# A new order table for an attention and channel-mix kernel: one batch's k'v in single PSUM banks, and a planner that keeps VectorE and GpSimd apart

## The chip, the cores and the metric

The kernel runs on one core of one Trainium2 chip. The metric is the device time of one execution in microseconds (us), the median of three runs; less is better. The time before is 196.96 us (196.91 to 197.13).

## The reference

For each of 8 batches and 8 heads, with 576 rows of 64 columns: q is put through a softmax along its 64 columns, k through a softmax along its 576 rows, then kv = k'v (64x64 for each head) and x = q kv. The heads are laid side by side to rows of 512 columns. Then comes a channel mix:

```
xk = mu_k * x + (1 - mu_k) * x_prev        # x_prev is x, one row later
xr = mu_r * x + (1 - mu_r) * x_prev
k  = max(xk @ w_k, 0)                      # 512 -> 1024
v  = (k * k) @ w_v                         # 1024 -> 512
out = v / (1 + exp(-(xr @ w_r)))           # w_r: 512 -> 512
```

Inputs and output are float32; the matrix products run in bf16.

## The kernel before, in words

The eight heads of a batch are worked on as two **units** of four heads, so "(1,0)" below is unit 0 of batch 1. The steps for a unit are: load q, k and v (L338, SP's queue); exponentials of q and k on ScalarE (L344); v to bf16 (`cast_v`, L349); the row sums of q with a reciprocal (`sum_q`, L354) and the multiply by it (`scale_q`, L359), both on VectorE; the transpose of q; k'v on TensorE (`kv`, L385, 36 small products over 64 rows that add up in PSUM); then x.

Batches 0 and 1 take a way of their own. Their q is transposed on TensorE (L370) and copied out by ScalarE or VectorE (L377). Their k'v is scaled by the normaliser and by mu in `weigh_kv` (L401, on VectorE, in two calls w=0 and w=1, of which the first also takes the reciprocal of the normalisers), and the "mixed" products (`x_mixed`, L411) give xk and xr at once. There are four of these for each unit, and each is copied out by ScalarE or VectorE (L432). From batch 2 on q is transposed by a DMA (L381), k'v is normalised in `norm_kv`, and xk and xr are made by ScalarE and VectorE (L451, L456).

The channel mix has 8 "up" steps for each batch (`up`, L463: a block of 128 columns of w_k; for batches 0 and 1 each is cut into four quarter steps of two products), a relu (L471) and a square (L476); for each block of 128 rows a "gate" (`gate`, L484, with w_r), a tanh (L490) and a "down" (`down`, L500, with w_v), and `finish` (L507) and a store.

The weights come in as float32 and are cast to bf16: w_k in eight column blocks (`cast_wk`, L322), w_r in two halves (`cast_wr`, L326), w_v in four (`cast_wv`, L329), each on ScalarE, VectorE or GpSimd, through one helper (L248), so that all casts and copies have the lines L250 (ScalarE) and L251 (VectorE, GpSimd).

PSUM has 8 banks: three double tiles of two banks ("two", L204) for k'v, transposes, mixed and up products, and two single banks ("one", L205) for gate and down products.

The order of the work is fixed by hand, in the table `ORDER` (L21). Each word is a step's number; a letter behind it chooses the engine (A ScalarE, D VectorE, G GpSimd) where there is a choice. The class `Plan` (L57) goes through the table, reckons a start for each step from costs written beside the steps (L552 on), gives out the PSUM and SBUF buffers (the one that is free first), and the steps are issued in the order of these starts. So the table sets the order on each engine and on SP's queue; on the chip every engine then runs its list in order and waits on semaphores. A step with `shares` set is one that the planner takes to be slower when a VectorE and a GpSimd step run at one time (L107 to L115).

The steps are written down once each, and each has one number in both tables.

Of the kernel before, what the change touches and what calls it, by code (L numbers as in the profile page):

```python
# [21 lines left out]
0 2 1 3 4 7 8 9 10 11 76 96 80 12 13 81 82 6 100 79G 5 77 78A 85 101 86 83A 87 102 14 104D 84A  # L22
88 97 98A 103A 99G 28 105 90 89A 91A 92 17G 93A 106 16G 108 107 114 109A 110 112 115A 365 366
15G 18D 111A 19 113D 27 24 367 136 378 379 368 373 376 377 29 369 371 21G 380 372 22G 374 140
375 94 95D 362 363 23A 30 360 361 393 400 32 394 141 31 364 398 401 20G 33 382 116 399 395 402
384 370D 383 385 396 120 387 389 386 397 390 381A 25D 121 34 388 26G 391 142 37 143D 118D 138D
574 584 40 122 123D 117 119G 575 139G 125 124A 585 126 144D 127 579 569 137 130 131A 128 129A
145 146 147 134 36D 135A 132 148 150 43 133A 426 428 149A 427 431 392D 41 151A 433 429 432 403D
434 404 570 406 407 430 405 444 435 442 38G 408 445 39G 580 420 42 422 411 35D 156 412 423 45
421 409 159 410 576 424 436A 415 417 443 413 173 439 157 160 440 577 418 44 176 437 438 446 441  # L30
586 46 416 177 158 571 419 587 175 154 162 447D 152 174 572 155A 581 613 190 163 425D 153A 161
414D 614 164 179 193 615 582 166 178 589 590 165 47 595 180 168 591 578 169 596 49 597 51 601
602 583 50 170 167 603 194 181 616 172 48 598 171 617 186 187 182 188 183 184 607 191 207 608
609 209 192 463 189 55 464 465 185 210 195 466 458 460 448 57 629 56 588 208 467D 211 461 599
459 462D 453 241 450 449 451 196 454 212 244 197 245 624 630 625 213 214 198 243 200 600 592 199
54 452D 455 204 53 201 593 202 610 634 203 206 456 205 611 242 215 52 635 221 457D 247 619 220
223 620 217 594 216 621 222 58 618 218 219 248 225 631 224 470 471 480 246 227 612 632 468 481
469 478 573 622 228 258 623 261 475 639 476 644 479 640 645 249 250 251 252 226 230 604 253 255
229 636 482A 473 231 254 474 257 605 485 649 256 486 65 650 64 232 637 61 262 233 238 626 472D
483 627 237 239 234 235 63 240 633 484 659 654 59 277 62 236 500 66 487D 275 278 60 292 501 498  # L40
499 495 477A 493 660 488 655 263 294 279 280 494 496 497D 259 489 293 661 503 295 504 490 491
662 276 296 505 628 298 260 299 264 265 492D 651 506 68 266 268 652 281 267 664 507D 641 282 665
674 606 272 638 269 663 271 270 642 675 273 274 283 284 285 286 67 288 656 646 657 289 290 679
291 502D 647 309 74 287 73 508 312 520 509 343 346 521 510 310 511 523 515 643 516 669 512D 680
525 347 297 658 69 311 513 524 514 313 670 526 681 315 300 75 344 305 684 306 316 682 518 70 302
685 666 307 72 301 345 519 314 308 648 667 671 694 527A 522A 695 304 317 71 303 328 318 349 672
689 683 517D 319 690 320 323 322 350 326 676 321 696 324 677 530 327 545 325 528 673 546 543 529
329 348 544 540 531 699 533 697 698 678 534 330 532D 538 704 541 539 700 351 332 333 356 691 705
653 706 535 357 358 352 692 353 536 724 707 331 725 359 714 715 547D 537A 334 354 668 335 542D
701 355 702 708 336 337 711 339 340 341 342 726 555 560 727 709 556 710 338 558 757 729 758 712  # L50
703 561 730 565 559 566 759 563 734 564 735 567D 693 548 553 550 719 760 551 554 557D 549 552D
720 721 728 722 723 713 716 717 718 562A 736 731 737 686 732 738 733 687 744 745 739 749 740 741
688 750 761 568 754 742 743 755 746 747 756 748 751 752 753
# [3 lines left out]
class Plan:  # L57
# [8 lines left out]
    TURN, SHARE = 0.25, {"DVE": 0.45, "POOL": 0.7}  # L66
# [7 lines left out]
    def step(self, eng, cost, fn=None, after=(), uses=(), lat=0.12, narrow=False, shares=False):  # L74
# [81 lines left out]
def kernel(  # L156
# [12 lines left out]
    nc = tc.nc  # L169
# [10 lines left out]
    PARTS = ((0, 5), (5, 4))  # L180

# [54 lines left out]
    def at(kind, *key):  # L236
        return bufs[kind][slot[(kind, *key)]["idx"]]
# [146 lines left out]

    def kv(b, u):  # L385
        ps, ek, vb = at("two", "kv", b, u), at("ek", b, u), at("vb", b, u)
        for j in range(J):
            for g in range(2):
                for h in range(2):
                    r = slice(64 * g, 64 * g + 64)  # L390
                    nc.tensor.matmul(ps[64 * h:64 * h + 64, g, 0:65],  # L391
                                     lhsT=ek[r, j, 64 * h:64 * h + 64], rhs=vb[r, j, h, :],
                                     start=(j == 0), stop=(j == J - 1))
# [7 lines left out]
    def weigh_kv(b, u, w):  # L401
        ps, rz, rows = at("two", "kv", b, u), inv_k(b, u), slice(2 * w, 2 * w + 2)
        if w == 0:
            nc.vector.reciprocal(out=rz, in_=ps[:, :, 64])
        for g in range(2):
            nc.vector.scalar_tensor_tensor(
                out=at("kvm", b, u)[:, rows, g, :], scalar=rz[:, g:g + 1],
                in0=ps[:, g, None, 0:64].to_broadcast((128, 2, 64)),
# [174 lines left out]
    for a in range(2):  # L583
        queue.append(dma(2.85, lambda a=a: load_wk(a), after=early[-1:], uses=[sl("k2", "w")]))
        for c in range(4):
# [3 lines left out]
                shares=True)  # L589
# [3 lines left out]
                        uses=[sl("xr", "w")], shares=True) for c in range(2)]  # L593
# [3 lines left out]
    for a in range(2):  # L597
        first.append(dma(2.75, lambda a=a: load_wv(a), uses=[sl("k2", "w")],
                         after=[*queue, *(ev["wk", i] for i in range(FT))]))
        for c in (2 * a, 2 * a + 1):  # L600
            ev["wv"].append(pl.step({"POOL": 1.2, "ACT": 1.05, "DVE": 0.62}, 0,
                                    lambda e, c=c: cast_wv(e, c), after=[first[-1]],
                                    uses=[sl("k2", "w")], shares=True))
# [6 lines left out]
    for n in range(B):  # L610
        for u in range(2):
# [5 lines left out]
            if n < NM:  # L617
# [4 lines left out]
                              shares=True)  # L622
                      for h in range(2)]
            else:
                vc = [pl.step("POOL", 1.3, lambda n=n, u=u: cast_v("POOL", n, u),
                              after=[ev["ld", "v", n, u]], uses=[vb, sl("ldv", n, u)],
                              shares=True)]
            p = pl.step("DVE", 1.57, lambda n=n, u=u: sum_q(n, u), after=[qe], uses=[eq])
            p = pl.step("DVE", 1.32, lambda n=n, u=u: scale_q(n, u), after=[p], uses=[eq, qs],
                        shares=True)  # L630
            if n < NM:
                s = sl("two", "qt", n, u)
# [8 lines left out]
            s = sl("two", "kv", n, u)  # L641
            p = pl.step("PE", T_NARROW, lambda n=n, u=u: kv(n, u), after=[ke, *vc],
                        uses=[ek, vb, s], lat=0.3, narrow=True)
            if n < NM:
                km = sl("kvm", n, u)
                nk = [p, ev["mu"]]
                for w in range(2):
                    nk.append(pl.step("DVE", 0.75 - 0.2 * w, lambda n=n, u=u, w=w: weigh_kv(n, u, w),
                                      after=nk, uses=[s, km, sl("mub")], lat=0.18))
                weighed += nk[2:]  # L650
                for w in range(2):
                    for c in range(2):
# [11 lines left out]
                         uses=[s, kn], lat=0.35)  # L664
# [15 lines left out]
    for b in range(B):  # L680
        relus = []
        for f in range(FT):
# [14 lines left out]
            if f % 2:  # L697
# [3 lines left out]
                                              lat=0.2, shares=True)  # L701
# [167 lines left out]
```

## Time and profile before

| | before |
|---|---|
| median of three runs | 196.96 us (196.91 to 197.13) |
| the profiled execution | 198.4 us |
| its span, first to last instruction | 196.6 us |
| mean granted TensorE clock | 0.991 |
| last link of the chain that ended last | the last down products on TensorE from 188.93 us, 3.65 us long, then VectorE, 0.42 us |

The profile comes from one execution of its own, so its span and the median of the runs are not the same time. Times in a timeline are microseconds from the span's start. A timeline row gives start, length, engine, line, operation, what is written and read, how many instructions, and in brackets how long the engine stood idle before it and what it waited for. PE is TensorE, DVE VectorE, ACT ScalarE, POOL GpSimd, SP the engine that issues most DMAs. Instructions of one engine overlap a little, so a row can start before the one ahead of it has ended.

### The profile page before, as it was taken

How to read it: one execution, taken by the hardware profiler on the slowest of the kernel's cores; microseconds unless marked ns; L12 is line 12 of the kernel's file. 1: busy time of each engine (PE TensorE's matmuls, PEld its weight loads, DVE VectorE, ACT ScalarE, POOL GpSimd, SP SyncE). 2: the span in 40 equal slices, each digit the busy share in tenths (PEclk: the TensorE clock that was granted, in tenths of full speed). 3: DMA queues.
4: the chain of work that ended last, by engine and by line, in shares of the span. 5: the costliest groups of instructions: out<-in, count | busy, mean ns of one | idle time of the engine just before them, and what ended most of it. 6: DMA issues, size and time to landing. Idle time of an engine off the chain costs nothing. (4 is left out here: it accounts for less than half of the span.)

```text
span 196.6 us, 4720 instructions
## 1 busy us (share of the span) xinstructions
PE 186.3 (95%) x1905; PEld 111.9 (57%) x1905; DVE 145.1 (74%) x225; ACT 144.7 (74%) x214; POOL 30.3 (15%) x40
## 2 busy tenths in 40 slices
PE   6699699999999999999999999999999999999991
PEld 4467475765546754665566645754576546664441
DVE  1984996669999997985997898998791688225222
ACT  3898779897799798887899686979956692752210
POOL 2024731533002312000115000152000000000000
PEclk9879999999999999999999999999999999999999
DMA  5999999994899999949995999948809325104824
GB/s 203 374 398 387 388 391 386 391 390 118 200 327 357 282 264 401 280 106 317 391 350 115 273 285 299 324 153 175 229 19 170 88 53 137 28 0 104 187 71 127
DMA packets 35896, 46.86 MB, mean 238 GB/s; under 512 B 16280, under 2 KB 16544, under 8 KB 35872
## 3 DMA queue, kind: packets, MB, share of 16 engines
q1 hardware_dynamic: 35456, 46.02, 77.8%
q10 hardware_dynamic: 416, 0.53, 1.0%
q8 instruction: 15, 0.25, 0.5%
q14 instruction: 9, 0.07, 0.1%
HBM read 33.56 MB, written 9.44 MB: 219 GB/s over the span
## 5 line engine op out<-in xcount | busy, mean ns | idle before, releaser
L467 PE MATMUL two<-xk,wk_bf 128*128 128x288 bf16 x512 | 66.8, 286 | 1.7 <-POOL wk_bf L251 1.7
L503 PE MATMUL one<-wv_bf,k 128*128 128x512 bf16 (+1 forms) x296 | 65.9, 374 | 0.1
L467 PEld LDWEIGHTS <-wk_bf 128*128 128x128 bf16 x512 | 49.8, 98 | 18.6 <-POOL wk_bf L251 2.0
L472 ACT ACTIVATE rel<-two 128x576 bf16<-128x576 f32 x64 | 40.2, 654 | 22.0 <-PE two L467 19.7
L503 PEld LDWEIGHTS <-k 128*128 128x128 bf16 x296 | 28.1, 98 | 31.0 <-issue 0.6
L486 PE MATMUL one<-wr_bf,xr 128*128 128x512 bf16 x144 | 35.9, 379 | 0.1
L251 POOL CAST vb<-ldv 128x1152 bf16<-128x1152 f32 (+1 forms) x16 | 19.8, 1237 | 92.2 <-DMA ldv<-in_v_dram 91.9
L453 ACT ACTIVATE aw<-two,om 128x575 bf16<-128x575 f32 x48 | 32.5, 748 | 1.5 <-PE two L445 1.5
L491 ACT ACTIVATE th<-one 128x512 f32<-128x512 f32 x36 | 21.5, 604 | 13.4 <-PE one L486 13.4
L509 DVE SCALAR_TENSOR_TENSOR ot<-th,one 128x512 f32<-128x512 f32 x33 | 22.2, 675 | 7.7 <-PE one L503 6.8
L360 DVE TENSOR_TENSOR qs<-eq,inv 128x1152 bf16<-128x1152 bf16 x16 | 25.6, 1607 | 0.2
L355 DVE TENSOR_REDUCE rs<-eq 128x18 f32<-128x1152 bf16 x16 | 21.5, 1346 | 5.2 <-ACT eq L345 5.1
L482 DVE TENSOR_TENSOR k<-rel 128x1152 bf16<-128x1152 bf16 x24 | 18.1, 766 | 8.2 <-ACT rel L472 8.2
L458 DVE SCALAR_TENSOR_TENSOR xk<-two,mu,aw 128x576 bf16<-128x576 f32 x24 | 19.3, 812 | 6.1 <-ACT aw L453 6.0
L486 PEld LDWEIGHTS <-xr 128*128 128x128 bf16 x144 | 13.5, 98 | 13.7 <-issue 0.9
L345 ACT ACTIVATE eq<-ldq 128x1152 bf16<-128x1152 f32 x16 | 18.6, 1170 | 2.7 <-DMA ldq<-in_q_dram 2.6
L458 DVE SCALAR_TENSOR_TENSOR xr<-two,mu,aw 128x576 bf16<-128x576 f32 x24 | 19.2, 810 | 1.4 <-ACT aw L453 1.4
L345 ACT ACTIVATE ek<-ldk 128x1152 bf16<-128x1152 f32 x16 | 18.9, 1181 | 0.0
L480 ACT ACTIVATE k<-rel 128x1152 bf16<-128x1152 bf16 x8 | 9.3, 1180 | 0.0
L333 PE MATMUL one<-ident 128*128 128x256 bf16 x31 | 6.8, 381 | 1.8 <-DVE halves L271 1.8
L391 PE MATMUL two<-vb,ek 64*64 64x65 bf16 x576 | 8.1, 197 | 0.1
L391 PEld LDWEIGHTS <-ek 64*64 64x64 bf16 x576 | 6.7, 110 | 2.3 <-issue 1.1
(56 smaller groups left out, 86.8 us busy)
## 6 DMA issues: line engine op xcount, KB each, us to landing
ldq<-in_q_dram SPq DMA_DIRECT2D x16, 576.0 KB, 7.1
ldk<-in_k_dram SPq DMA_DIRECT2D x16, 576.0 KB, 7.0
out_dram<-ot SPq DMA_DIRECT2D x66, 128.0 KB, 2.7
ldv<-in_v_dram SPq DMA_DIRECT2D x14, 576.0 KB, 7.7
k<-in_moe_w_k_dram SPq DMA_DIRECT2D x2, 1024.0 KB, 12.9
k<-in_moe_w_v_dram SPq DMA_DIRECT2D x2, 1024.0 KB, 12.5
ldv<-in_v_dram SPq DMA_DIRECT2D x4, 288.0 KB, 8.6
xr<-in_moe_w_r_dram SPq DMA_DIRECT2D x1, 1024.0 KB, 14.2
```

Source lines behind the costliest of these rows:

```text
L251: return {"DVE": nc.vector, "POOL": nc.gpsimd}[eng].tensor_copy(out=out, in_=in_)
L345: nc.scalar.activation(out=at("e" + n, b, u)[:].rearrange("p j (h d) -> p h j d", h=2), in_=at("ld" + n, b, u)[:].rearrange("p h (j d) -> ...
L355: nc.vector.reduce_sum(out=rs[:], in_=at("eq", b, u)[:].rearrange("p j (h d) -> p (j h) d", h=2), axis=AX.X)
L360: nc.vector.tensor_tensor(out=at("qs", b, u)[:].rearrange("p j (h d) -> p (j h) d", h=2), in0=at("eq", b, u)[:].rearrange("p j (h d) -> p ...
L453: nc.scalar.activation(out=at("aw", b, u, h, w)[:, 1:S], in_=x_of(b, u, h)[:, 1:S], func=ACT.Copy, scale=om[:, c:c + 1])
L458: nc.vector.scalar_tensor_tensor(out=blend(b, w)[:, 2 * u + h, :], in0=x_of(b, u, h)[:, 64:64 + S], scalar=mu[:, c:c + 1], in1=at("aw", b, ...
L467: nc.tensor.matmul(ps[:, a, 0:HS], lhsT=wk_bf[:, ct, 128 * f:128 * f + 128], rhs=xk[:, ct, HS * a:HS * a + HS], start=(ct == 0), stop=(ct ...
L472: nc.scalar.activation(out=at("rel", b, f // 2)[:, f % 2, :].rearrange("p (a c) -> p a c", a=2), in_=at("two", "up", b, f)[:, :, 0:HS], fu ...
L486: nc.tensor.matmul(at("one", "rp", i, m)[:], lhsT=at("xr", i)[:, ct, 128 * m:128 * m + 128], rhs=wr_bf[:, ct, :], start=(ct == 0), stop=(c ...
L491: nc.scalar.activation(out=at("th", i, m)[:], in_=at("one", "rp", i, m)[:], func=ACT.Tanh, scale=0.5)
L503: nc.tensor.matmul(at("one", "vp", i, m, a)[:, cols], lhsT=at("k2", i)[:, f, 128 * m:128 * m + 128], rhs=wv_bf[:, f, cols], start=(f == 0) ...
L509: nc.vector.scalar_tensor_tensor(out=at(kept(i, m), i, m)[:, cols], in0=at("th", i, m)[:, cols], scalar=1.0, in1=at("one", "vp", i, m, a)[ ...
```

## The change

There are three edits. First, the k'v of unit 1 of batch 1 goes to the two single banks in place of one double tile, a bank for each pair of heads; the reciprocal of its two normalisers is then two instructions in place of one:

```diff
+    KV_SINGLE = (1, 1)
...
+    def kv_of(b, u, g):
+        if (b, u) == KV_SINGLE and ("one", "kv", 0) in slot:
+            return bufs["one"][g][:, 0:65]
+        return at("two", "kv", b, u)[:, g, 0:65]
...
     def weigh_kv(b, u, w):
...
+        if w == 0 and (b, u) != KV_SINGLE:
+            nc.vector.reciprocal(out=rz, in_=at("two", "kv", b, u)[:, :, 64])
+        elif w == 0:
+            for g in range(2):
+                nc.vector.reciprocal(out=rz[:, g:g + 1], in_=ps[g][:, 64:65])
```

Second, in the planner, a VectorE and a GpSimd step of the sharing kind no longer slow each other by a share of their common time; the later one in the table starts when the other has ended. Only the last sharing step of each engine is looked at:

```diff
-    TURN, SHARE = 0.25, {"DVE": 0.45, "POOL": 0.7}
+    TURN = 0.25
...
-            if s["shares"] and e in sharing:
+            if e in s["shares"]:
                 sharing[e], other = s, sharing["POOL" if e == "DVE" else "DVE"]
-                both = min(other["end"], t + cost) - max(other["start"], t) if other else 0.0
-                if both > 0.0:
-                    cost += self.SHARE[e] * both
-                    longer = self.SHARE[other["on"]] * both
+                if other and other["start"] <= t:
+                    t = max(t, other["end"])
+                elif other and other["start"] < t + cost:
+                    longer = t + cost - other["start"]
                     other["cost"] += longer
                     other["end"] += longer
                     busy[other["on"]] += longer
```

The casts of v for batches 0 and 1 now count as sharing on GpSimd only. Third, the table is a new one. Of its 762 steps none is added or dropped. These are the two orders where the first batches are worked on (x is a mixed product, weigh the two calls w=0 and w=1, "exp q (1,0)" the exponential of q).

| engine | before | after |
|---|---|---|
| TensorE, up products of batch 0, in quarter steps | blocks 1, 3, 2, then x (0,0) w=1 c=1, 0, then 6, 7, 4, 5 mixed | all x of batch 0 first; blocks 0, 2, 3, 1, then 7 three times, 6, 7, 5, 6, 6, 6, 5, 5, 5, 4 four times |
| TensorE, from there to the up products of batch 1 | transposes (1,1), gates 1, 3, transposes (1,0), k'v (1,0), gates 2, 0, two x of (1,0), k'v (1,1), two x of (1,0), two x of (1,1) | gates 0, 3, transposes (1,0), gate 1, k'v (1,0), gate 2, transposes (1,1), two x of (1,0), k'v (1,1), two x of (1,0), two x of (1,1) |
| VectorE, same stretch | w_k block 3, copy of x, sum (1,1), copy of x, multiply (1,1), square, sum (1,0), half of w_r, multiply (1,0), copy of q, two casts of v, copy of q, weigh (1,0) around a copy of q, weigh (1,1), quarter of w_v, two squares, quarter of w_v | w_k block 3, two copies of x, w_k blocks 7 and 4, sum and multiply (1,0), half of w_r, sum and multiply (1,1), cast of v, two copies of q, weigh (1,0), two copies of q, weigh (1,1) w=0, copy of x, square, quarter of w_v, weigh (1,1) w=1, square |
| GpSimd | v, v, w_k blocks 2, 1, 0, 5, 6, 4, half of w_r, v, v, two quarters of w_v | v, v, v, w_k blocks 1, 0, 5, 6, half of w_r, v, v, v, three quarters of w_v |
| ScalarE, w_k | block 7 | block 2 |
| SP's loads | q (1,1), w_k second half, q (1,0), w_r, k, v (1,0), v, k, v (1,1), w_v first, second half | q (1,0), w_k second half, q (1,1), w_r, k, v (1,0), k, v, v (1,1), w_v second, first half |

Behind that stretch the order of up, gate, down and k'v steps, of squares (some on the other of ScalarE and VectorE) and of stores, loads and DMA transposes on SP's queue differs in many places. Counted by step, VectorE has 178 before and 179 after, ScalarE 211 and 209, GpSimd 27 and 28. TensorE's 64-row steps (k'v, x, mixed) stand in 20 runs in both tables: 15 of them behind the first up products of batch 1 before, 16 after.

More of the change, by code (lines that the diff above doesn't have):

```diff
@@ L28 @@
[L28 to L33, printed above, removed]
@@ L72, in slot, with step @@
         return {"kind": kind, "users": 0, "idx": None, "end": 0.0}
-    def step(self, eng, cost, fn=None, after=(), uses=(), lat=0.12, narrow=False, shares=False):
+    def step(self, eng, cost, fn=None, after=(), uses=(), lat=0.12, narrow=False, shares=()):
         s = {"eng": eng if isinstance(eng, dict) else {eng: cost}, "fn": fn, "lat": lat,
@@ L401, in weigh_kv @@
     def weigh_kv(b, u, w):
-        ps, rz, rows = at("two", "kv", b, u), inv_k(b, u), slice(2 * w, 2 * w + 2)
-        if w == 0:
-            nc.vector.reciprocal(out=rz, in_=ps[:, :, 64])
+        ps, rz, rows = [kv_of(b, u, g) for g in range(2)], inv_k(b, u), slice(2 * w, 2 * w + 2)
+        if w == 0 and (b, u) != KV_SINGLE:
[3 more added lines that the diff above has]
+                nc.vector.reciprocal(out=rz[:, g:g + 1], in_=ps[g][:, 64:65])
         for g in range(2):
@@ L592 @@
                         lambda e, c=c: cast_wr(e, c), after=[queue[-1]],
-                        uses=[sl("xr", "w")], shares=True) for c in range(2)]
+                        uses=[sl("xr", "w")], shares=("DVE", "POOL")) for c in range(2)]
     first = [ld(n, 1, u, early[-1:]) for n, u in (("q", 0), ("q", 1), ("k", 0), ("v", 0), ("k", 1))]
@@ L640 @@
                              uses=[qs, qT], lat=3.3)]
-            s = sl("two", "kv", n, u)
+            if (n, u) == KV_SINGLE:
+                kv_at = [sl("one", "kv", g) for g in range(2)]
+            else:
+                kv_at = [sl("two", "kv", n, u)]
             p = pl.step("PE", T_NARROW, lambda n=n, u=u: kv(n, u), after=[ke, *vc],
-                        uses=[ek, vb, s], lat=0.3, narrow=True)
+                        uses=[ek, vb, *kv_at], lat=0.3, narrow=True)
             if n < NM:
@@ L647 @@
                 for w in range(2):
-                    nk.append(pl.step("DVE", 0.75 - 0.2 * w, lambda n=n, u=u, w=w: weigh_kv(n, u, w),
-                                      after=nk, uses=[s, km, sl("mub")], lat=0.18))
+                    nk.append(pl.step("DVE", (0.92 if (n, u) == KV_SINGLE else 0.75) * (1 - w) + 0.55 * w, lambda n=n, u=u, w=w: weigh_kv(n, u, w),
+                                      after=nk, uses=[*kv_at, km, sl("mub")], lat=0.18))
                 weighed += nk[2:]
```

78 lines of the change are left out of this document (42 added, 36 removed).

## The prediction

> **What bounds the kernel now.** I read the page first, then busy time by stretches, then the timelines of the engines where TensorE is not full.
>
> ```profile
> span 196.6 us, 4720 instructions
> ...
> PE 186.3 (95%) x1905; PEld 111.9 (57%) x1905; DVE 145.1 (74%) x225; ACT 144.7 (74%) x214; POOL 30.3 (15%) x40
> ```
>
> ```profile
> 17.00:24.00 7.00, 5.25 (x56) 3.67 (x46) 5.35 (x7) 5.76 (x9) 3.57 (x5) 1.00 1.05 387
> 24.00:35.60 11.60, 11.38 (x196) 7.62 (x195) 9.60 (x20) 9.44 (x15) 2.86 (x4) 1.00 1.05 388
> 35.60:47.00 11.40, 11.40 (x84) 7.83 (x82) 7.93 (x10) 10.33 (x15) 6.02 (x4) 1.00 0.92 331
> 47.00:68.00 21.00, 20.86 (x225) 11.94 (x223) 20.83 (x30) 18.66 (x27) 2.50 (x2) 1.00 0.93 265
> ...
> 100.00:150.00 50.00, 50.00 (x521) 30.86 (x520) 42.99 (x61) 40.58 (x60) 7.97 (x5) 1.00 0.80 215
> ```
>
> The columns are length, busy PE, PEld, DVE, ACT, POOL, clock, DMA share, GB/s. From 35.6 us on TensorE has no hole worth naming (11.40 of 11.40, 20.86 of 21.00, 50.00 of 50.00), at full clock. So a new order can win almost nothing there. It can win in the stretch 17 to 24 (5.25 of 7.00), and it can lose anywhere. The timeline of TensorE around that hole:
>
> ```profile
> 20.54 1.15 PE L467 MATMUL two<-xk,wk_bf 128*128 128x288 bf16 x8
> 23.42 4.09 PE L467 MATMUL two<-xk,wk_bf 128*128 128x288 bf16 x32 [1.73 <-POOL wk_bf L251]
> 27.35 0.67 PE L374 MATMUL two<-ident,qs 128*128 128x128 bf16 x9
> 27.86 1.89 PE L486 MATMUL one<-wr_bf,xr 128*128 128x512 bf16 x8
> 29.58 0.67 PE L374 MATMUL two<-ident,qs 128*128 128x128 bf16 x9
> 30.21 0.48 PE L391 MATMUL two<-vb,ek 64*64 64x65 bf16 x36
> 30.70 2.00 PE L486 MATMUL one<-wr_bf,xr 128*128 128x512 bf16 x8
> 32.63 0.69 PE L423 MATMUL two<-qT,kvm 64*64 64x256 bf16 x20
> 33.27 0.48 PE L391 MATMUL two<-vb,ek 64*64 64x65 bf16 x36
> 33.73 0.41 PE L423 MATMUL two<-qT,kvm 64*64 64x256 bf16 x8
> 34.32 1.29 PE L423 MATMUL two<-qT,kvm 64*64 64x320 bf16 x32 [0.18 <-ACT xk L250]
> 35.59 0.65 PE L467 MATMUL two<-xk,wk_bf 128*128 128x288 bf16 x4
> ```
>
> At 21.69 TensorE stops for 1.73 us until GpSimd has cast a column block of w_k. Then it runs the second half of batch 0's up products, and from 27.35 the transposes, gates 0 to 3 and batch 1's first mixed products. At 35.59 batch 1's up products begin. Both tables put the same 59 TensorE steps ahead of that point. So I measure the change there: **the start of batch 1's up products, 35.59 now.** TensorE is full from there to the end, and a shift of that start passes into the time one for one.
>
> The wait has its cause on two engines. GpSimd's rows, then VectorE's:
>
> ```profile
> 15.58 0.87 POOL L251 CAST wk_bf<-k 128x512 bf16<-128x512 f32 x1 [2.03 <-DMA k<-in_moe_w_k_dram]
> 20.99 0.61 POOL L251 CAST wk_bf<-k 128x512 bf16<-128x512 f32 x1 [3.43 <-DMA k<-in_moe_w_k_dram]
> 21.55 1.82 POOL L251 CAST wk_bf<-k 128x512 bf16<-128x512 f32 x1
> 25.19 1.04 POOL L251 CAST wr_bf<-xr 128x1024 bf16<-128x1024 f32 x1 [0.74 <-DMA xr<-in_moe_w_r_dram]
> ```
>
> ```profile
> 15.55 0.43 DVE L251 CAST wk_bf<-k 128x512 bf16<-128x512 f32 x1
> 21.55 1.34 DVE L360 TENSOR_TENSOR qs<-eq,inv 128x1152 bf16<-128x1152 bf16 x1
> 22.81 1.16 DVE L482 TENSOR_TENSOR k<-rel 128x1152 bf16<-128x1152 bf16 x1
> 23.90 1.34 DVE L355 TENSOR_REDUCE rs<-eq 128x18 f32<-128x1152 bf16 x1
> 25.27 0.27 DVE L357 RECIPROCAL inv<-rs 128x18 f32<-128x18 f32 x1
> 25.45 1.32 DVE L251 CAST wr_bf<-xr 128x1024 bf16<-128x1024 f32 x1
> 26.70 1.34 DVE L360 TENSOR_TENSOR qs<-eq,inv 128x1152 bf16<-128x1152 bf16 x1
> ```
>
> GpSimd's 0.61 us cast took 1.82 beside a VectorE multiply: it ended at 23.37, 0.48 after the multiply (22.89). VectorE's next step, the square at 22.81, ended 0.60 after that cast. VectorE's cast of w_r ended 0.54 after GpSimd's (26.23). So the two take turns, the one that waits goes next, and a blocked step needs 0.48 (GpSimd, 512 columns) or 0.54 (VectorE, 1024) more.
>
> **The change part by part.** *The wait at 21.69.* The two w_k halves and w_r land at these times:
>
> ```profile
> 6.16 2.18 SPq L309 DMA_DIRECT2D k<-in_moe_w_k_dram  x1
> ...
> 10.92 1.24 SPq L314 DMA_DIRECT2D xr<-in_moe_w_r_dram  x1
> ```
>
> ```profile
> DMA to landing us min/median/max: 11.0/12.9/14.8
> ...
> DMA to landing us min/median/max: 14.2/14.2/14.2
> ```
>
> Second half of w_k: 6.16 + 14.8 = 20.96; w_r: 10.92 + 14.2 = 25.12. The moved loads ahead of w_r (q of batch 1, units swapped) have one size, so I keep both. The new table casts blocks 7 and 4 on VectorE, 5 and 6 on GpSimd, and TensorE takes 7 first. In turns: block 7 at 20.98 + 0.43 = 21.4; 5 at 21.9; 4 (0.28, the 0.43 less the 0.15 that a blocked cast saves, to 0.43) at 22.2 to 22.3; 6 at 22.6 to 22.8. TensorE has the same work before (the eighth mixed product, now at 20.20, moves ahead of the up products), arrives at about 21.8, does three quarter steps of block 7 (4.09/16 = 0.253 each), waits at most 0.3 for block 6, and ends batch 0 at about 26.0. Gain here: 27.35 - 26.0, about 1.3.
>
> *Gates first.* Next in the old order is a transpose that needs no w_r; in the new one gate (0,0), which needs both halves of w_r. One engine's cast runs after the other's, whichever begins: 25.19 + 1.04 + 0.54 = 26.77. TensorE starts the gate at about 26.85. **0.8 of the 1.3 is given back**: its lead is 27.35 - 26.85 = 0.5.
>
> *VectorE's chain.* Now VectorE has, between the landings, two casts, a row sum, its reciprocal and a multiply of unit (1,0): 20.98 + 0.43 + 0.48 + 0.28 + 1.35 + 0.27 + 1.36 = 25.15, to 25.3 with 0.43. Its cast of w_r is next, and GpSimd's is issued at 25.19. There is no slack; anything late lets GpSimd go first. I take GpSimd first: VectorE's cast ends at 26.77, sum and reciprocal of (1,1) at 28.35. Then:
>
> ```profile
> 28.21 0.68 POOL L251 CAST vb<-ldv 128x576 bf16<-128x576 f32 x1 [1.98 <-DMA ldv<-in_v_dram]
> ```
>
> ```profile
> 28.13 0.49 DVE L251 COPY qT<-two 128x640 bf16<-128x640 bf16 x1
> 28.54 1.40 DVE L251 CAST vb<-ldv 128x576 bf16<-128x576 f32 x2
> ...
> 31.57 0.16 DVE L404 RECIPROCAL inv<-two 128x2 f32<-128x2 f32 x1
> 31.76 0.61 DVE L406 SCALAR_TENSOR_TENSOR kvm<-two,inv,mub 128x128 bf16<-128x128 f32 x2
> ```
>
> The multiply of (1,1) waits for GpSimd's cast of v (28.89) and ends at 30.2. Only then comes VectorE's cast of half of v (0.74, not slowed beside GpSimd at 28.54), to 30.9. TensorE by start-to-start distances (gate 0.86, transposes 0.63, k'v 0.46, mixed 0.3 to 0.4): gates to 28.6, transposes 29.2, gate 30.05, **a wait of 0.85 for that cast**, k'v of (1,0) to 31.4, gate 32.25, transposes 32.9, two mixed 33.65, k'v of (1,1) to 34.1, two mixed 34.7. The scaled k'v of (1,1) needs two reciprocals and two multiplies, 0.32 + 0.61, from 34.2: 35.1. Two mixed products, then up at about 35.8. **Sum: 35.8 - 35.59 = +0.2.**
>
> *The single banks.* One more reciprocal (0.16) is in that sum. Freeing a double tile is worth at most the 0.18 wait at 34.32. The banks must first be freed by the tanh of gate (0,2):
>
> ```profile
> 30.04 0.61 ACT L491 ACTIVATE th<-one 128x512 f32<-128x512 f32 x1
> ```
>
> 32.25 + 0.1 + 0.6 = 32.95, hidden behind two mixed products (to 33.65); without them it would cost 0.7. They are next used by the down product after 22 quarter steps (5.6 us): hidden, since the last reader on VectorE is about 3 us of steps behind. If that reader were over 2 us late, the down product and all behind it on TensorE would wait.
>
> *The rest of the table.* One more run of 64-row products in the full stretch: k'v alone is 0.49 (30.21 to 30.70), among others 0.46, so 0.03 at least; with its entry I take 0.1. Squares change engine (VectorE 178 to 179 steps, ScalarE 211 to 209). On SP the late loads, stores and transposes change place, by a few issues each; the transposes of batch 2 come one issue earlier. All of this costs nothing while TensorE is full, and TensorE's products are the cover; every gap there is new cost. Bounds: below, the 0.14 hole in 47 to 68 closes; above, one more wait like the 0.85 worked out here. I take +0.1.
>
> Sum: +0.2 + 0.1 + 0.1 = +0.4. The profiled execution took 198.4 with its span of 196.6, so span 197.0 and about 198.8 with a profile. The median of the runs is 196.96, 0.36 above the span, so **197.4**; this case alone, 197.0 to 197.7.
>
> **The rivals.** *VectorE first, faster.* If the multiply of (1,0) ends by 25.16, VectorE casts w_r at 25.16 to 25.85, and its chain is 0.9 earlier: cast of v at 29.5, k'v of (1,0) at 30.0 without a wait, (1,1) at about 33.3, up at 35.1. That is -0.45 + 0.1: 196.6 (196.3 to 196.9). For it: at 15.55 VectorE started 0.03 before GpSimd at one landing, and kept its 0.43 while GpSimd's 0.61 became 0.87. Against it: the sum 25.15 to 25.3 has hardly room. In the Trainium skill, "SBUF — State Buffer", section "Who interferes with whom", the port pair that both share is held for a whole instruction, and "Issue order, not op shape, decides who blocks". The trace agrees (1.82 us beside 1.34); by that rule this case holds if VectorE's cast is issued before 25.19.
>
> *A new hole later.* VectorE is busy 20.83 of 21.00 us in 47 to 68. If it enters that stretch late or the new order asks for a step too early, TensorE waits. One wait of the 0.85 kind: 198.2. Against it: VectorE had 3.5 idle us in 35.6 to 47.
>
> *The wait simply goes.* If nothing is given back, 196.96 - 1.73 + 0.1 = 195.3; with only the gates' 0.8 given back, 196.1. Against it: VectorE's cast of w_r, 1.32 instead of about 0.6.
>
> *The change does not do what it says.* Its exclusion is a rule of the planner; on the chip only order, engines and banks change. Then the time is a matter of the table, which the sum covers.
>
> **How the numbers follow.** Forecast 0.45, VectorE first 0.30, a later hole 0.15, the wait simply goes 0.10. The range 196.3 to 198.3 leaves out the last and the far ends. A measurement here tells about 0.2% (0.39 us) from no change: slower means above 197.35 (0.25 of the forecast's 0.45, and the later hole: 0.40), faster below 196.57 (0.12 of the second and the last: 0.22), the rest 0.38.
>
> **What would show it.** Right: no wait at block 6 over 0.3; the first gate at 26.8 behind the cast of w_r; VectorE's cast of w_r over 1.2 us; a wait of TensorE before k'v of (1,0); batch 1's up products at 35.6 to 36.0; TensorE full afterwards. Wrong: VectorE's cast of w_r at 0.69 and up products at 35.1; or any wait over 0.3 after 36 us.

## The result, and the profile after

| | before | after |
|---|---|---|
| median of 22 runs each | 197.19 us (196.85 to 198.95) | 198.26 us (197.42 to 201.13) |
| ratio, with its 95% interval | 1 | 1.0051 (1.003 to 1.0072) |
| profiled execution: time, span | 198.4 us, 196.6 us | 198.23 us, 195.8 us |

The ratio leaves out one slow execution of after, that of 201.13 us. The change makes the kernel about 1.1 us slower. Yet the profiled execution of after is the shorter one. So those two profiles alone would tell the wrong story. The cause is the profile of before, as a further run of the same kernel (ctl_before, below) shows. First the page of after, then its busy time by stretches (length, busy PE, PEld, DVE, ACT, POOL, clock, DMA share, GB/s), cut at its own events:

```profile
span 195.8 us, 4722 instructions
...
PE 186.3 (95%) x1905; PEld 111.6 (57%) x1905; DVE 145.4 (74%) x227; ACT 145.1 (74%) x212; POOL 27.7 (14%) x41
```

```profile
24.00:33.72 9.72, 9.26 (x180) 5.92 (x178) 8.21 (x19) 9.31 (x15) 4.43 (x5) 1.00 1.04 388
33.72:47.00 13.28, 12.98 (x88) 8.49 (x87) 11.60 (x15) 12.08 (x16) 4.30 (x4) 1.00 1.04 342
47.00:68.00 21.00, 20.66 (x299) 11.78 (x298) 18.78 (x30) 18.73 (x28) 4.68 (x4) 1.00 1.10 293
100.00:150.00 50.00, 50.00 (x554) 29.87 (x552) 42.31 (x64) 40.38 (x60) 5.85 (x5) 1.00 0.84 231
```

TensorE works the same 186.3 us, and it is no longer full behind the start of batch 1's up products: it lacks 0.30 us in 33.72 to 47 and 0.34 in 47 to 68. TensorE's timeline of after:

```profile
17.40 8.10 PE L476 MATMUL two<-xk,wk_bf 128*128 128x288 bf16 x64
25.33 2.19 PE L495 MATMUL one<-wr_bf,xr 128*128 128x512 bf16 x8
27.35 0.67 PE L375 MATMUL two<-ident,qs 128*128 128x128 bf16 x9
...
33.72 1.14 PE L476 MATMUL two<-xk,wk_bf 128*128 128x288 bf16 x8
35.15 1.02 PE L476 MATMUL two<-xk,wk_bf 128*128 128x288 bf16 x7 [0.30 <-DVE xk L252]
```

Batch 0's 64 up products run without a hole, the gates begin at 25.33, and batch 1's up products at 33.72, where the profile of before had 35.59. After eight of them TensorE waits 0.30 us for VectorE. VectorE's and GpSimd's casts of w_r answer the question that the prediction left to a knife edge:

```profile
22.98 1.36 DVE L361 TENSOR_TENSOR qs<-eq,inv 128x1152 bf16<-128x1152 bf16 x1
24.41 0.70 DVE L252 CAST wr_bf<-xr 128x1024 bf16<-128x1024 f32 x1
```

```profile
24.44 1.56 POOL L252 CAST wr_bf<-xr 128x1024 bf16<-128x1024 f32 x1 [2.59 <-DMA xr<-in_moe_w_r_dram]
```

VectorE was first by 0.03 us and kept its 0.70; GpSimd's 1.04 became 1.56.

### The profile page after: what moved, and what is told of

It reads as the page before. It is cut to its first block, busy times and chain, and to the rows that moved or that the text cites. A ratio compares the mean times of both kernels' runs of the same rounds, so it can differ in the third digit from the quotient of the medians.

```text
span 195.8 us, 4722 instructions
## 1 busy us (share of the span) xinstructions
PE 186.3 (95%) x1905; PEld 111.6 (57%) x1905; DVE 145.4 (74%) x227; ACT 145.1 (74%) x212; POOL 27.7 (14%) x41
## 5 line engine op out<-in xcount | busy, mean ns | idle before, releaser
L476 PE MATMUL two<-xk,wk_bf 128*128 128x288 bf16 x512 | 67.6, 286 | 0.3 <-DVE xk L252 0.3
L252 POOL CAST vb<-ldv 128x1152 bf16<-128x1152 f32 (+1 forms) x18 | 18.5, 1027 | 101.0 <-DMA ldv<-in_v_dram 79.6
L491 DVE TENSOR_TENSOR k<-rel 128x1152 bf16<-128x1152 bf16 x23 | 19.6, 852 | 11.1 <-ACT rel L481 11.1
L361 DVE TENSOR_TENSOR qs<-eq,inv 128x1152 bf16<-128x1152 bf16 x16 | 23.3, 1457 | 0.3
L489 ACT ACTIVATE k<-rel 128x1152 bf16<-128x1152 bf16 x9 | 10.5, 1167 | 0.2
L397 PE MATMUL two<-vb,ek 64*64 64x65 bf16 x540 | 7.4, 197 | 0.2 <-POOL vb L252 0.2
```

What stands on the lines that cost most here:

```text
L361: nc.vector.tensor_tensor(out=at("qs", b, u)[:].rearrange("p j (h d) -> p (j h) d", h=2), in0=at("eq", b, u)[:].rearrange("p j (h d) -> p ...
L476: nc.tensor.matmul(ps[:, a, 0:HS], lhsT=wk_bf[:, ct, 128 * f:128 * f + 128], rhs=xk[:, ct, HS * a:HS * a + HS], start=(ct == 0), stop=(ct ...
L491: nc.vector.tensor_tensor(out=dst, in0=r[:], in1=r[:], op=ALU.mult)
```

## The experiments

All ran on the kernels' own inputs. The last four columns are read from each run's one profile (the stretch from batch 1's first up product to the end of TensorE's last matmul, and the tail from there to the end of the span) and from all its executions (time minus span). The ratio is not the quotient of the two medians.

| run | median us | ratio to before, 95% interval | stretch | tail | time - span, median | above 2.15 |
|---|---|---|---|---|---|---|
| ctl_before | 196.96 | 1.0008 (0.9982 to 1.0033) | 156.87 | 4.0 | 1.83 | 0 of 12 |
| ctl_after | 198.30 | 1.0062 (1.0041 to 1.0084) | 157.49 | 4.4 | 2.30 | 8 of 12 |
| f_pool_first | 198.28 | 1.0051 (1.0022 to 1.008) | 157.71 | 4.4 | 1.87 | 5 of 12 |
| f_dve_first | 198.90 | 1.0101 (1.0056 to 1.0147) | 157.96 | 4.3 | 2.21 | 4 of 6 |
| t_store_first | 198.29 | 1.0041 (1.0012 to 1.007) | 157.21 | 4.0 | 1.98 | 0 of 12 |
| h_copy_act | 197.74 | 1.002 (0.9989 to 1.0052) | 156.87 | 4.4 | 2.00 | 0 of 12 |
| g_sum_late | 199.82 | 1.0117 (1.0062 to 1.0171) | 159.17 | 4.4 | 1.89 | 2 of 5 |
| p_pad | 198.05 | 1.0042 (1.0006 to 1.0078) | 157.49 | 4.3 | 1.79 | 0 of 12 |
| c_all | 197.65 | 1.0013 (0.9992 to 1.0035) | 157.28 | 4.0 | 1.81 | 0 of 12 |
| q_before_pad | 197.04 | 0.9999 (0.9973 to 1.0025) | 156.98 | 4.0 | 1.96 | 0 of 12 |
| k_pool_later | 198.56 | 1.0065 (1.0034 to 1.0097) | 157.20 | 4.4 | 2.33 | 9 of 10 |
| e_rule_alone | 197.33 | 1.0013 (0.9989 to 1.0037) | 156.87 | 4.0 | 1.99 | 0 of 12 |

The kernel before had 196.97 to 197.11 in the runs beside them. Its time minus span was 1.74 to 1.95 in every one of those, with a median of 1.82.

### Both kernels again, and the order of the two casts

ctl_before and ctl_after are the two kernels unchanged. The other two are meant to make one engine first at w_r:

```diff
 # f_pool_first: VectorE comes later
+    pad = const.tile([128, 512], F32, name="pad")
...
+        if eng == "DVE":
+            nc.vector.memset(pad[:], 0.0)
 # f_dve_first: GpSimd comes later
+    pad = const.tile([128, 512], F32, name="pad")
...
+        if eng == "POOL":
+            nc.gpsimd.tensor_copy(out=pad[:, 0:64], in_=wr_raw()[:, 2 * c, 0:64])
```

> The kernel before against itself. Every theory: ratio 1.000. It gives the span and the time beside each other for the old order, where the new order's profiled execution had a span of 195.8 us (0.8 less than the old one's 196.6) at a time of 198.23 (1.0 more than the median of before). If what lies outside the span is the same 1.8 to 2.4 us for both orders, spans of about 195 for the old one; if the new order adds something outside the span, spans as those of the new one.

> The changed kernel as it is. Theory 1 (GpSimd's cast of w_r goes first in most executions, VectorE first in the profiled one): ratio about 1.005, and batch 1's up products start more than 10.4 us after w_r's landing in a typical profile. Theory 2 (VectorE first nearly always, the loss lies behind 36 us): ratio about 1.005, that start 9.3 to 9.9 us after the landing, and TensorE waits later on that the old order has not.

> The changed kernel with a memset of 128x512 on VectorE ahead of its cast of w_r, so that GpSimd's cast goes first. Theory 1 (most executions are so already): the time of the changed kernel within 0.3 us. Theory 2 (VectorE goes first as a rule): 0.6 to 1.0 us slower than the changed kernel, with batch 1's up products at 10.4 us or more behind w_r's landing.

> The changed kernel with a copy of 64 columns on GpSimd ahead of its cast of w_r, which waits for the same landing, so that VectorE's cast goes first. Theory 1: 0.6 to 0.9 us faster than the changed kernel, about 0.998 of the kernel before. Theory 2: the time of the changed kernel within 0.3 us.

The pair repeats the loss: 198.30 - 196.97 = 1.33 us. The timeline of ctl_before around the wait on which the prediction built its gain:

```profile
20.32 1.74 POOL L251 CAST wk_bf<-k 128x512 bf16<-128x512 f32 x3 [2.85 <-DMA k<-in_moe_w_k_dram]
...
20.99 5.07 PE L467 MATMUL two<-xk,wk_bf 128*128 128x288 bf16 x40
...
21.79 1.48 DVE L360 TENSOR_TENSOR qs<-eq,inv 128x1152 bf16<-128x1152 bf16 x1
...
34.14 1.61 PE L467 MATMUL two<-xk,wk_bf 128*128 128x288 bf16 x11
```

And its busy time by stretches, the two behind the start of batch 1's up products (columns as above), in which TensorE has no hole:

```profile
34.10:47.00 12.90, 12.90 (x91) 8.54 (x88) 9.39 (x13) 11.65 (x17) 4.58 (x4) 1.00 1.09 349
47.00:68.00 21.00, 21.00 (x260) 12.31 (x259) 20.25 (x29) 18.09 (x28) 3.66 (x3) 1.00 1.01 291
```

There is no wait of 1.73 us. The second half of w_k landed earlier, so that GpSimd began its three casts at 20.32 and not at 20.99, and was through at 22.06; VectorE's multiply met only the last of them. In the first profile it had come in among them at 21.55 and made 3.46 us of 1.74. **The gain that was to be had was in that one execution, of 198.4 us, and not in this one, near the median.** Batch 1's up products began at 34.14 here, not at 35.59. The wait isn't the same in all executions: of the two other profiles with the old table (runs below), e_rule_alone has none and q_before_pad has 0.56 us of it, in two parts.

Theory 1, that GpSimd first makes the loss, falls: in ctl_after VectorE was first (25.00, GpSimd 25.03), batch 1's up products began 9.3 us behind that, as theory 2 had it, and the loss is there. f_pool_first did not do what it was meant to, at least in its profiled execution:

```profile
24.99 0.48 DVE L330 MEMSET pad<- 128x512 f32 x1
...
25.05 1.87 POOL L253 CAST wr_bf<-xr 128x1024 bf16<-128x1024 f32 x1 [2.59 <-DMA xr<-in_moe_w_r_dram]
25.39 0.63 DVE L253 CAST wr_bf<-xr 128x1024 bf16<-128x1024 f32 x1
```

VectorE's memset began 0.06 us before GpSimd's cast, and VectorE's cast came right behind it and was not held up: it ended at 26.02, GpSimd's at 26.92. So its median, 198.28, says nothing of GpSimd first. In f_dve_first VectorE was first as meant (24.67, GpSimd's cast 25.41), and the time was not better (198.90, of six runs, with the added copy in it); neither theory had that.

What the order is worth is seen better where nothing was forced: in the profiles of the runs below VectorE was first in three of the new table's, GpSimd in three (t_store_first, g_sum_late, c_all). From batch 0's first up product to batch 1's first it is 16.0 to 16.3 us with GpSimd first, and 15.9 to 16.7 us with VectorE first (these three, after and ctl_after). So the order hardly matters in these. But in the three with GpSimd first batch 0's up products also began later, at 18.89 to 20.03 and not at 17.40 to 18.26. What GpSimd first would cost in an execution with an early start no run shows.

Theory 2, a loss behind 36 us, holds for half: ctl_after's stretch is 0.62 us longer. The rest is in its tail (0.4) and outside its span (2.30 - 1.82 = 0.48). The start gains nothing. Between the two profiled executions, 198.53 and 196.95 us, the difference is made up of 0.16 in the start (34.30 - 34.14), 0.62 in the stretch, 0.4 in the tail and 0.4 outside the span.

### Where the stretch, the tail and the end lose

New theories were needed. Theory A: these are separate small holes, each passed on to the end. Theory B: they lie beside other work, or belong together in another way. The new hole, the wait of TensorE for VectorE that ends at 35.15, has this before it in the timeline of after:

```profile
33.53 0.63 ACT L251 CAST xk<-two 128x512 bf16<-128x512 f32 x1
...
33.72 1.14 PE L476 MATMUL two<-xk,wk_bf 128*128 128x288 bf16 x8
34.00 1.21 ACT L489 ACTIVATE k<-rel 128x1152 bf16<-128x1152 bf16 x1
34.27 0.82 DVE L252 CAST xk<-two 128x640 bf16<-128x640 f32 x1 [1.41 <-ACT xk L251]
```

VectorE now has one of the two copies into xk, and it stands idle for 1.41 us until ScalarE's copy into another part of the same tile ends (33.53 + 0.63 = 34.16). The tails of ctl_before and ctl_after:

```profile
187.37 3.63 PE L503 MATMUL one<-wv_bf,k 128*128 128x256 bf16 x24
187.42 0.69 DVE L509 SCALAR_TENSOR_TENSOR last<-th,one 128x512 f32<-128x512 f32 x1 [3.87 <-PEq L833]
...
188.14 4.13 ACTq L519 DMA_DIRECT2D out_dram<-last  x5
```

```profile
188.16 3.63 PE L512 MATMUL one<-wv_bf,k 128*128 128x256 bf16 x24
188.21 0.69 DVE L518 SCALAR_TENSOR_TENSOR last<-th,one 128x512 f32<-128x512 f32 x1 [3.87 <-PEq L845]
189.30 0.42 DVE L518 SCALAR_TENSOR_TENSOR last<-th,one 128x256 f32<-128x256 f32 x1 [0.41 <-PE one L512]
...
189.75 3.35 ACTq L528 DMA_DIRECT2D out_dram<-last  x5
```

ACTq is ScalarE's DMA queue. Before, its first store is issued at 188.14, behind VectorE's first finish (188.11). After, it is issued at 189.75, behind the second (189.72), though the first ended at 188.90: the new table puts the store of half of block (3,8), the last 128 rows of the last two batches, ahead of block (3,6)'s, and that one waits behind it. Then the end: the DMA view of ctl_after, in a window that lies behind its span of 196.2, shows an instruction fetch; ctl_before's has no packet behind its span.

```profile
DMA packets 1, 0.01 MB, mean 1 GB/s; under 512 B 0, under 2 KB 0, under 8 KB 0
...
q14 instruction: 1, 0.01, 0.4%
```

Each of these got its own run (general() is the kernel's other branch, for normalisers out of range, which is not taken here), and the steps of VectorE behind 46 us one as well:

```diff
 # t_store_first: the end of the table
-747 752 756 743 748 753
+747 752 743 756 748 753
 # h_copy_act
     def evict_mixed(eng, b, u, w, c):
-        copy(eng,
+        copy("ACT" if (b, u, w, c) == (1, 1, 0, 0) else eng,
 # g_sum_late: 193, the row sums of q (3,0), from behind 157 to behind 582
 # p_pad: in general(), which isn't executed
+        for n in range(124):
+            nc.vector.memset(mx[:], 0.0)
+        for n in range(3):
+            nc.scalar.copy(out=mkb[:], in_=identf[:])
```

> The changed kernel with one word of the table moved: the store of block (3,6) ahead of the store of block (3,8), half 1, so that ScalarE's queue issues its stores in the order of VectorE's finishes again; nothing else differs. Theory A (the loss behind 36 us is a sum of separate small holes, each passed on to the end): from TensorE's last matmul to the end of the span 4.05 us instead of 4.37 to 4.40, ScalarE's first store right behind VectorE's first finish, and the time 0.33 us below the changed kernel, about 1.0 us above the kernel before. Theory B (the holes lie beside other work): the last store ends as late as it did, the tail stays at 4.4 and the time within 0.1 us of the changed kernel.

> The changed kernel with one copy moved: ScalarE, not VectorE, copies the 640-element part of batch 1's second unit into xk, as it does in the kernel before; buffers and everything else stay. Theory A: the wait of the up products of that unit falls from 0.46 us to 0.15 or less, the way from batch 1's first up product to the last matmul from 157.5 to 157.75 to about 157.2 to 157.4, and the time falls by 0.3 to 0.35 us. Theory B: ScalarE's square, which now stands 0.6 us later, is late for what follows, the hole reappears behind it, and the time stays within 0.1 us.

> The changed kernel with one step of VectorE moved: the row sums of q for batch 3's first unit (1.35 us, with its reciprocal 0.27) behind the finishes of blocks (0,0) and (0,2), not ahead of k'v of (2,0). Theory A: the two waits of the gate at 50.3 to 51.4 us (0.3 us together, 0.5 in the other profile) go, and the time falls by 0.3 us. Theory B: the scaling of q for batch 3 and its transposes come 1.6 us later, the wait comes back in front of batch 3's products, and the time stays within 0.1 us or rises.

> The changed kernel with 124 memsets on VectorE and 3 copies on ScalarE added inside the branch that isn't taken: they don't execute; they only move the end of these two engines' programs, to the place modulo 128 instructions where the kernel before has it. Theory A (the additional 0.4 to 0.5 us outside the span in most executions of the changed kernel is the instruction fetch behind the program's end, and where the end lies decides it): time minus span is 1.75 to 1.95 us in every execution, as in the kernel before, no fetch comes behind the end, the span stays at 195.8 to 196.4, and the median time falls by 0.3 to 0.4 us. Theory B (it goes with something else in the changed kernel): time minus span is still 2.2 to 2.45 in half of the executions or more.

*t_store_first.* The tail as expected: 4.0.

```profile
189.62 3.63 PE L512 MATMUL one<-wv_bf,k 128*128 128x256 bf16 x24
189.67 0.69 DVE L518 SCALAR_TENSOR_TENSOR last<-th,one 128x512 f32<-128x512 f32 x1 [3.87 <-PEq L845]
...
190.39 4.15 ACTq L528 DMA_DIRECT2D out_dram<-last  x5
```

The store follows the first finish again (190.36). The time fell by less than the 0.33: it is 1.18 us above the kernel before beside it, where ctl_after was 1.33 above, and its spans, 195.2 to 197.3, scatter more than that. The tail's loss is shown by the trace, not by the median. Its stretch is short, 157.21, for another reason, the order of two steps that is told next: VectorE was first there (50.89, GpSimd 50.95), and its square took 0.75.

*h_copy_act.* More than expected: the stretch is 156.87, the figure of the kernel before to 0.01 us, and the median is 0.63 above the kernel before, not 1.33. The wait at 35 is gone, but so is the one at 50. The reason is in two rows of its timeline, beside the two of after:

```profile
48.56 0.75 DVE L491 TENSOR_TENSOR k<-rel 128x1152 bf16<-128x1152 bf16 x1
48.58 1.75 POOL L252 CAST vb<-ldv 128x1152 bf16<-128x1152 f32 x1 [5.11 <-DMA ldv<-in_v_dram]
```

```profile
48.41 1.17 POOL L252 CAST vb<-ldv 128x1152 bf16<-128x1152 f32 x1 [5.24 <-DVE inv L403]
48.53 1.65 DVE L491 TENSOR_TENSOR k<-rel 128x1152 bf16<-128x1152 bf16 x1
...
50.10 1.27 DVE L518 SCALAR_TENSOR_TENSOR ot<-th,one 128x512 f32<-128x512 f32 x2
...
50.83 0.98 PE L495 MATMUL one<-wr_bf,xr 128*128 128x512 bf16 x3 [0.33 <-DVE ot L518]
```

In the profiles of the new table VectorE's square and GpSimd's cast of v begin within 0.02 to 0.46 us of each other, now one first, now the other, and the second pays: GpSimd 1.75 for 1.17, which nobody waits for, or VectorE 1.65 for 0.75. Behind the square stand the finishes that free a bank, and TensorE's gate waits for that bank. ctl_before has no cast of GpSimd there. So about half of the shorter stretch, the wait at 35, is the moved copy's, and the other half is luck: in c_all, below, the same copy is moved, and GpSimd was first. The median is no measure of the copy either, since 0.3 us of what it fell by lies outside the span (2.00 for 2.30).

*g_sum_late* made it worse, as theory B had it. Its waits of TensorE:

```profile
PE two L454 <- DVE kvs L404: 1.1, 1, 1.1
PE one L495 <- DVE ot L518: 0.6, 1, 0.6
```

The square was second again:

```profile
50.09 1.17 POOL L252 CAST vb<-ldv 128x1152 bf16<-128x1152 f32 x1 [5.47 <-DMA ldv<-in_v_dram]
```

```profile
50.11 1.74 DVE L491 TENSOR_TENSOR k<-rel 128x1152 bf16<-128x1152 bf16 x1
```

The row sums, now at 52.97 and 1.6 us long with their reciprocal, pushed VectorE's normalising of the next k'v back, for which TensorE then waited 1.1 us. No other place for them was tried.

*p_pad.* Time minus span is 1.75 to 1.93 in all twelve, with no fetch behind the end, and the median is 0.94 above the kernel before, not 1.33. Its stretch is that of ctl_after. So the fetch, and the longer time outside the span, go with where the two programs end.

### All at once, the end's place in the kernel before, the collision, the rule

```diff
 # c_all: the edits of t_store_first and h_copy_act, and in general()
+        for n in range(125):
+            nc.vector.memset(mx[:], 0.0)
+        for n in range(2):
+            nc.scalar.copy(out=mkb[:], in_=identf[:])
 # q_before_pad: the kernel before, in general()
+        for n in range(4):
+            nc.vector.memset(mx[:], 0.0)
+        for n in range(125):
+            nc.scalar.copy(out=mkb[:], in_=identf[:])
 # k_pool_later: in cast_v
+        if (b, u) == (2, 1):
+            nc.gpsimd.tensor_copy(out=at("vb", b, u)[:, 0:4, 0, 0:64],
+                                  in_=at("ldv", b, u)[:, 0, 0:256].rearrange("p (j d) -> p j d", d=D))
 # e_rule_alone: the table of the kernel before, and
-    KV_SINGLE = (1, 1)
+    KV_SINGLE = (-1, -1)
```

> The changed kernel with three of its losses taken back at once: the store of block (3,6) first again, the 640-element copy into xk of batch 1's second unit on ScalarE again, and unexecuted instructions in the branch that isn't taken (125 on VectorE, 2 on ScalarE) that put the ends of the two programs where the kernel before has them modulo 128. Theory A (the whole loss is these places): from batch 1's first up product to the last matmul 156.9 us, tail 4.05, time minus span 1.75 to 1.95, and the median within 0.2 us of the kernel before (196.8 to 197.3). Theory B (there is a further loss, in the start or elsewhere, or the three don't add): 0.5 us or more above the kernel before.

> The kernel before, with 4 memsets on VectorE and 125 copies on ScalarE inside the branch that isn't taken: nothing of it executes, but these two programs now end where those of the changed kernel end, modulo 128 instructions. Theory A (the end's place decides whether one more instruction block is fetched behind it): time minus span is 2.2 to 2.45 us in half of the executions or more, where the kernel before has 1.75 to 1.95 in all, and the median rises by 0.2 to 0.45 us. Theory B (it belongs to something else in the changed kernel): time minus span stays at 1.75 to 1.95 and the time within 0.1 us.

> The changed kernel with GpSimd's cast of v for batch 2's second unit preceded by a cast of 256 of its elements (written again by the whole cast), so that the whole cast begins some 0.35 us later, behind the start of VectorE's square at 48.5 to 49.1 us. Theory A (the gate's waits at 50.3 to 51.4 come from the order of these two: whoever comes second waits for the other): VectorE's square takes 0.75 to 1.1 us instead of 1.39 or 1.65, the waits at 50 to 52 fall below 0.1 us, the wait at 35 stays, and the way from batch 1's first up product to the last matmul is 157.2 us. Theory B (VectorE's queue is too long there in any order, and the moved copy at 35 was what helped): the waits stay at 0.3 us.

> One part of the change alone: the planner's new rule of exclusion with the table of the kernel before, and k'v of batch 1's second unit in a double bank as before. The orders of the engines are the old ones but for steps that the plan starts at nearly the same time, and some buffers rotate differently. Theory A (the loss is in the new table's places): the time lies within 0.3 us of the kernel before. Theory B (what the rule does to buffers and to the order in which steps are issued costs by itself): 0.5 us or more above it.

*c_all* is level with the kernel before, 1.0013 (0.9992 to 1.0035), and doesn't beat it; but its median is 0.56 higher, which is theory B's case and not theory A's 0.2. Tail and end are back (4.0, 1.81). The further loss is in the stretch, 0.41 longer, because here GpSimd was first again:

```profile
49.32 1.16 POOL L252 CAST vb<-ldv 128x1152 bf16<-128x1152 f32 x1 [5.13 <-PE two L432]
...
49.63 1.45 DVE L491 TENSOR_TENSOR k<-rel 128x1152 bf16<-128x1152 bf16 x1
...
51.73 0.59 PE L495 MATMUL one<-wr_bf,xr 128*128 128x512 bf16 x2 [0.21 <-DVE ot L518]
```

*k_pool_later* settles that collision: VectorE's square kept its 0.75, TensorE had no wait for a finish, and the stretch is 157.20, as theory A had it. What is left over 156.87 is the hole at 35 (0.33). Its median, 198.56, doesn't show the gain: its spans, 195.5 to 197.3, scatter by more than that. The gain is shown by the trace alone.

```profile
49.01 1.01 POOL L353 CAST vb<-ldv 128x256 bf16<-128x256 f32 x1 [5.16 <-DMA ldv<-in_v_dram]
49.01 0.75 DVE L494 TENSOR_TENSOR k<-rel 128x1152 bf16<-128x1152 bf16 x1
```

*q_before_pad* got the fetch behind the end, and time minus span rose to a median of 1.96 (1.77 to 2.09), by 0.14 and not by 0.3 or more; the time didn't move. With p_pad and c_all this shows that the fetch comes and goes with the place of the end. That the fetch itself makes the longer time is not shown. e_rule_alone has a median of 1.99, 0.17 above the kernel before, and its profiled execution (2.02) has no packet behind its span of 195.2:

```profile
DMA packets 0, 0.00 MB, mean 0 GB/s; under 512 B 0, under 2 KB 0, under 8 KB 0
```

The four profiled executions above 2.15 (after, ctl_after, g_sum_late, k_pool_later) all have the fetch. But h_copy_act and t_store_first have it too, and no execution above 2.15; and f_pool_first and f_dve_first, with five of 12 and four of 6 above 2.15, have none in their profiled executions of 1.85 and 1.89. What makes the end long stays open.

*e_rule_alone* lies within 0.3 us (0.24, of which 0.17 is outside the span), with the stretch and the tail of the kernel before: the planner's rule by itself costs nothing that can be told. The single banks by themselves were not tried, so what they cost is not told apart from the new table.

## Why the prediction was right, and where it was not

The direction and the range held (slower, 198.26 in 196.3 to 198.3), 0.04 us inside the range's upper edge. The forecast's own case, 197.0 to 197.7, did not come, and the working held less well.

- *TensorE is full behind 35.6, and a shift passes one for one.* Right for the kernel before: in the four profiles of the old table the stretch is 156.87 to 156.98, with its start at 34.14 to 35.59. For the new table it failed: I had listed any wait over 0.3 us behind 36 as a sign against me, and after has one of 0.33 at 50.83. The +0.1 for gaps in the rest of the table was 0.62 in ctl_after and 0.88 in after (157.75). **This is the step that was mis-sized.** The rival "a new hole later", 198.2 at 0.15, is what came, but not by its own ground, a VectorE without room in 47 to 68 (20.83 of 21.00): in after VectorE is busy for 18.78 there, and the holes came from a copy that waited for ScalarE's and from a square that waited for GpSimd's cast.
- *The wait at 21.69, gain 1.3.* The mechanism was read rightly, and after has no wait at block 6. But ctl_before has none either, and q_before_pad 0.56. Against the median the term is about nothing. The sum was made on a span of 196.6, while the executions near the median had 195.2, and time minus span is 1.8, not the 0.36 between the profile's span and the median of other executions.
- *Gates first, 0.8 back.* Wrong: in after and ctl_after the gates began at 25.33 and 25.74, right behind batch 0's up products. VectorE's half was done by then (25.11, 25.69), GpSimd's was not (26.00, 26.59), and only the gate's second half waited for it, 0.31 us in ctl_after. Where GpSimd was first, in c_all and g_sum_late, the gates began at 26.75 and 26.74, near the 26.85 of the sum, but for another reason: batch 0's up products had begun 1.3 us later than in ctl_after, and TensorE shows no wait there.
- *VectorE's chain.* The knife edge was rightly found: in after the multiply ended at 24.34 and the cast of w_r began at 24.41, 0.03 ahead of GpSimd's. But I took GpSimd first, and VectorE was first in after and ctl_after, with the 0.70 that I had listed as a sign against me. There was no wait before k'v of (1,0) in these two, and batch 1's up products began at 33.72 and 34.30, not at 35.8. The case that I took is seen in c_all and g_sum_late: VectorE's cast took 1.53 us, and the wait for its cast of v came, but with 0.22 and 0.31 us and not 0.85; the up products began at 35.09 and 35.16. So the condition of the rival "VectorE first" was met, but its 196.6 didn't come: ctl_before has 34.14 already, and the losses lay behind.
- *The single banks.* Right as far as the profiles show: in after and ctl_after TensorE has no wait for these banks.
- *One more run of 64-row products, +0.1.* Nothing: h_copy_act, with all runs of the new table, has the 156.87 of the kernel before.
- *Not in the sum at all:* the tail (0.4) and the time outside the span (0.48). The prediction speaks only of SP's stores, as different "by a few issues each", and costs them at nothing; the one that lost time is on ScalarE's queue.

A gain that wasn't there and losses that weren't counted left the sum near the result. That the number lies in the range is luck, not a proof of the working.

## What to carry to other kernels

Take a second profile of the kernel before when the first one's time is not its median's: a wait that depends on who comes first by 0.1 us can be in one execution and not in the next, and no gain can be built on it. When an order of steps changes, look at the last few stores as closely as at the first loads, and at every pair of VectorE and GpSimd steps that come due together, above all where VectorE is the one for whom others wait. And find for each tile that two engines write who waits for whom. Where an edit is to force an order, read in its trace whether it did.

## What the runs showed of the hardware

Whoever comes second of VectorE's square and GpSimd's cast of v waits, and 0.02 us decide it. In h_copy_act the square, 0.02 us ahead, took 0.75 us and the cast 1.75; in g_sum_late the square, 0.02 us behind, took 1.74 and the cast 1.17. In all seven profiles in which the cast was first, with a lead of 0.02 to 0.46 us, the square ended 0.59 to 0.61 us behind the cast's end, so a smaller lead costs VectorE more. The Trainium skill, "SBUF — State Buffer", section "Who interferes with whom", says that issue order decides who blocks; the trace agrees in these rows.

One instruction block was fetched behind the span's end in some kernels, and instructions that are never executed took the fetch away (p_pad, c_all) or brought it (q_before_pad). The median time outside the span went with it, from 2.30 to 1.79 in p_pad and from 1.82 to 1.96 in q_before_pad.

TensorE's granted clock in the head differs between executions. The stretches 12 to 15.4 and 15.4 to 18.4 us (columns as above) of t_store_first, and the second of ctl_after:

```profile
12.00:15.40 3.40, 2.87 (x63) 2.26 (x66) 1.53 (x7) 2.54 (x4) 1.83 (x3) 0.50 1.05 401
15.40:18.40 3.00, 3.00 (x78) 1.75 (x74) 2.23 (x7) 1.41 (x3) 1.17 (x2) 0.50 1.05 388
```

```profile
15.40:18.40 3.00, 2.57 (x59) 1.94 (x60) 1.75 (x4) 2.83 (x5) 1.43 (x2) 1.00 1.05 387
```

At half the clock, in t_store_first, batch 0's up products began at 20.03 instead of 17.64, and batch 1's at 36.05 instead of 34.30. Against such a difference between two executions, 1.75 us, a gain of 0.3 us can be read in a trace here, and hardly in a median of twelve runs.
